# Steps of the second and third token block put in another order (chunked attention followed by an ELU feed-forward, one core)

## The chip, the cores and the metric

The kernel runs on one core of a Trainium2 chip. The metric is the device time of one execution in microseconds (us), taken as the median of several runs. One more execution was recorded by the hardware profiler; the views of that profile are what is read below.

## The reference

What has to be computed, cut to its core (float32 throughout; 8 batches, 8 heads, 576 positions of 64 numbers, so 4608 tokens of 512 numbers; `w_in` is 512x2048, `w_out` 2048x512):

```
scores = scale * q_c @ k_c.T            # per head, inside chunks of 64 positions
attn   = exp(scores - max(scores))
attn   = attn / (sum(attn) + 1e-9)
x      = (attn @ v_c)                   # written as [4608 tokens, 512]
h      = x @ w_in
g      = where(h > 0, h, exp(min(h, 0)) - 1)
out    = g @ w_out
```

Every float32 product of the feed-forward is made of three matmuls of rounded parts: a high part and a low part of each operand, without low times low. Where the text says that something is "split", its high part is a copy on ScalarE and its low part a subtraction on VectorE or GpSimd.

## The kernel before, in words

**Blocks.** The 4608 tokens are nine blocks of 512 (`TB`). The first three are done plainly: `hidden(f)` computes 128 of the 2048 hidden numbers for all 512 tokens with 12 matmuls of 128x512 into a PSUM tile `h` (two buffers); `elu` turns `h` into `ghi` and `glo`; `second_products()` multiplies those with `w_out` in 12 more matmuls into four PSUM tiles `o`, one step later than `hidden` (the queue behind `second`). `f` runs from 0 to 15 in each block. The other six blocks are done as three pairs with seven products for eight (a Strassen scheme: `Pair`, `PAIR`, `KEPT`). They need sums and differences of token blocks, made by `prepare`: B11, B21, B22 are split parts of x, and T1 to T4 are split differences of x of block three and block four. t1, t2, t3, t4 are the bare differences, T1 to T4 their splits. The ending `a` or `b` on such a name means the first columns up to `T2`, or the rest; a token tile is 128 columns, so `T2 = 256` is two tiles of block four and `T2 = 384` three.

**Attention in between.** While block b is in the feed-forward, the attention of later tokens is worked in tiles of 128 (class `Later`): `turn(0)` and `turn(1)` transpose q and k on VectorE (`qT`, `k_turned`), `score` is 32 small matmuls into the PSUM tile `ps_a`, `less_max` two VectorE steps, `exp` one ScalarE step, `sums` three VectorE steps, `turn_a` two VectorE steps, a ScalarE copy (`unturned`) and four DMAs on SyncE's queue, `times_v` 32 small matmuls into `ps_a`, `keep` a ScalarE copy into `xf`.

**What sets the order.** Each engine runs its instructions in the order in which the code issues them; nothing is moved by a scheduler. That order stands in strings, one letter per step, which the loops read from left to right:

- In blocks one and two: `H` is `hidden(f)`, each `e` one of the four parts of `elu` (1: relu and exp on ScalarE; 2: the combining step on VectorE, line 442; 3: `ghi` on ScalarE; 4: `glo`), `P` the 12 products into `o`, `a` the next step of the tile begun earlier, `n` the next step of the following tile, `S` the storing of the finished block, `X` the splitting of x for the next block into `xhi` and `xlo`.
- In block three (`EVEN`, `ODD`, `THIRD_BLOCK`): `q`, `k` are `turn(0)` and `turn(1)`, `s` score, `m` or `M` less_max, `E` or `F` exp, `z` sums, `h` turn_a, `v` times_v, `x` keep, `l` and `V` the loads of a following tile, `A1` to `A7` loads of weight sums, and `xB11`, `xt1a`, `xT1a` and so on a `prepare`.

A letter that is already done for its tile is skipped. An instruction waits for what it reads and for the space that it writes, and all that stands behind it on its engine waits with it. In block three `glo` runs on GpSimd from f = 2 on. `combine()` is a side job that writes sums of weights to memory, one step at the end of each f.

The lines that the text speaks of: 422 the matmuls, 249 `score`, 257 `times_v`, 439 and 440 relu and exp of `elu`, 442 its combining step, 447 `ghi`, 450 `glo`, 455 and 456 the copy and the DMA of an output, 348 the transpositions of q and k, 358 and 359 `less_max`, 364 `exp`, 369 to 371 `sums`, 377 to 387 `turn_a`, 408 `keep`, 508 and 509 the split inside `combine`, 574 and 575 the split and 580 the difference in `prepare`, 847 and 848 the split of x (`split_next`), 636 and 640 the first steps on a product of a pair.

Of the kernel before, what the change touches and what calls it, by code (L numbers as in the profile page):

```python
# [20 lines left out]
def kernel(  # L21
# [19 lines left out]
    nc = tc.nc  # L41

    B, H, S, D = q.shape
# [4 lines left out]
    P = 128  # L48
    C = 64
    TB = 512  # L50
    NB = NT // TB
    NTT = TB // P
    NK = DM // P
    NF = DFF // P
    SCALE = 1.0 / float(D) ** 0.5
    Q = 32
# [1 line left out]
    NS = (NB - PLAIN) // 2  # L58
    NG = NF // 2
    LAG = 1  # L60
    T2 = TB // 2

    REBIAS = 2.0 ** -112
    LARGEST = float(np.uint32(0x0FEFFFFF).view(np.float32))
# [363 lines left out]
    def hidden(f: int):  # L428
        hi, lo = w_in_slices(f)
        h = ps_h.tile([P, TB], F32, name="h")  # L430
        for kt in range(NK):
            three(h, hi[:, kt, :], lo[:, kt, :], xhi[:, kt, :], xlo[:, kt, :],
                  kt == 0, kt == NK - 1)
        return h

    def elu(h, engine=nc.vector):

        e = gp.tile([P, TB], F32, name="e")
        nc.scalar.activation(out=e, in_=h, func=AF.Relu, scale=-1.0)  # L439
        nc.scalar.activation(out=e, in_=e, func=AF.Exp, scale=-1.0)  # L440
        yield
        nc.vector.scalar_tensor_tensor(  # L442
            out=e, in0=e, scalar=-1.0, in1=h, op0=ALU.add, op1=ALU.max
        )
        yield
        ghi = gp.tile([P, TB], F32R, name="ghi")
        nc.scalar.copy(out=ghi, in_=e)  # L447
        yield
        glo = gp.tile([P, TB], F32R, name="glo")
        engine.tensor_tensor(out=glo, in0=e, in1=ghi.bitcast(F32), op=ALU.subtract)  # L450
        yield ghi, glo

    def copy_out(o, n0: int, src, on_vector: bool):

        (nc.vector.tensor_copy if on_vector else nc.scalar.copy)(out=o, in_=src)  # L455
        nc.sync.dma_start(out=out[n0:n0 + P, :], in_=o)

    def store(blk: int, o_ps):
        for tt in range(NTT):
            o = io.tile([P, DM], F32, name="q_sb" if tt % 2 else "k_sb")  # L460
            copy_out(o, blk * TB + tt * P, o_ps[tt], tt % 2 and blk)

# [8 lines left out]
    PRODUCTS = {1: ("A11", "B11"), 2: ("A12", "B21"), 3: ("S4", "B22"), 4: ("A22", "T4"),  # L471
                5: ("S1", "T1"), 6: ("S2", "T2"), 7: ("S3", "T3")}
    a_dram = dram.tile([NG, P, 2, NA, 2 * P], F32, name="a_dram")
# [86 lines left out]
    def b_operand(name: str):  # L560
        place, i = {"B11": (0, 0), "B21": (0, 1), "T1": (1, 0), "T2": (1, 1), "T4": (2, 0),
                    "B22": (3, 0), "T3": (4, 0)}[name]
# [4 lines left out]
    def prepare(name: str, cols=slice(TB), engine=nc.vector):  # L567


        b11, b21, b12, b22 = [xf[:, t, 2 * k:2 * k + 2, cols] for t in range(2) for k in range(2)]  # L570
        sources = {"B11": b11, "B21": b21, "B22": b22, "T1": b11, "T2": b11, "T3": b12, "T4": b21}
        if name in sources:
# [98 lines left out]
    def o_tiles():  # L671
        return [ps_o.tile([P, DM], F32, name=f"o{tt}") for tt in range(NTT)]
# [46 lines left out]
    def warm(n: int):  # L719
# [19 lines left out]
    )  # L739
    SECOND_BLOCK = (  # L740
# [4 lines left out]
    )  # L745
# [1 line left out]
        "H e e e e P",  # L747
        "H e e e e P",
        "n n H e e e e P",
        "n a a n H n X P e e e e",  # L750
    )

    EVEN, ODD = "l H q k e e e e P", "H s v e x V m E e e z h e P"
    THIRD_BLOCK = {
# [9 lines left out]
    }  # L766
    FIRST_PAIR = (
# [40 lines left out]
    with (  # L808
# [5 lines left out]
        for item in LOADS.split():  # L814
            kind, n = item[0], int(item[1:])
# [26 lines left out]
    ps_early = early.enter_context(  # L842
        tc.tile_pool(name="ps_early", bufs=1, space=bass.MemoryType.PSUM))

    def split_next():
        for kt in range(NK):
            nc.scalar.copy(out=xhi[:, kt], in_=xf[:, 0, kt])
            nc.vector.tensor_tensor(  # L848
                out=xlo[:, kt], in0=xf[:, 0, kt], in1=xhi[:, kt].bitcast(F32), op=ALU.subtract)
# [19 lines left out]
    combining = combine()  # L869
# [3 lines left out]
    for blk in range(PLAIN - 1):  # L873
        if blk == 1:
            early.close()
            ps_a = ctx.enter_context(
                tc.tile_pool(name="ps_a", bufs=1, space=bass.MemoryType.PSUM))
        run = blk * TB, o_tiles(), None
        for f in range(NF):
            tt, st = divmod(f, 4)  # L880
            n = (blk + 1) * NTT + tt + 1
            if st == 0:
                if (blk, tt) == (1, 0):
                    following = later[2 * NTT].steps()
                tile_now, following, begun = following, iter(()), 0
                if blk:
                    next(tile_now, None)
                    next(tile_now, None)
                    if tt == 0:
                        later[n] = Later(n)  # L890
                        later[n].load_qk()
                    later[n].load_v()
                    following = later[n].steps()
            lines = FIRST_BLOCK if blk == 0 else SECOND_BLOCK if (blk, tt) == (1, 0) else LATER
            for item in lines[st].split():
                if item == "H":
                    if blk == 0:
                        split_upto(f)
                        if f == NF - 1:
                            kept_st += [stp.tile([P, STAGE], F32, name="kept", tag="st")  # L900
                                        for _ in range(3)][::-1]
                            later[2 * NTT] = Later(2 * NTT)
                            later[2 * NTT].load_qk()
                            later[2 * NTT].load_v()
                    act, acted = elu(hidden(f)), 0
                elif item == "e":
                    g, acted = next(act), acted + 1
                    if acted == 4:
                        second(f, *g)
                elif item == "a":  # L910
                    next(tile_now, None)
                    begun += 1
                    if begun == 2 and n < 2 * NTT:
                        following = early_tile(n)
                elif item == "n":
                    next(following, None)
                elif item == "d":
                    next(splitting, None)
                elif item == "r":
                    next(preparation, None)  # L920
                elif item == "X":
                    if f == NF - 1:
                        split_next()
                elif item == "P":
                    if blk or f:
                        second_products()
                elif item == "S":
                    store(*unstored.pop())
            if (blk or f > 1) and (not blk or f < 2):
                write_lo((f - 2) % NF)  # L930
            if blk:
                next(combining, None)
                if st == 2:
                    later[n + 1] = Later(n + 1)
                    later[n + 1].load_qk()

    n = PLAIN * NTT
    attention = Tokens(later[n], later[n + 1])
    attention.done |= {(n, item) for item in "qksmEV"}

    def do(item: str):
        if item == "Q":
            second_next()
        elif item == "P":
            second_products()
        elif item == "S":
            store(*unstored.pop())
        elif item[0] == "x" and len(item) > 1:
            if preparing:
                name, cols = item[1:3], slice(TB)  # L950
                if item[1] == "B":
                    name = item[1:4]
                elif item[3:4] in ("a", "b"):
                    cols = slice(T2) if item[3] == "a" else slice(T2, TB)
                prepare(name, cols)
        elif item[0] == "A":
            load_a(0, int(item[1]))
        else:
            attention.step(item)
# [3 lines left out]
    for f in range(NF):  # L963
        for item in THIRD_BLOCK.get(f, ODD if f % 2 else EVEN).split():
            if item == "H":
                act, acted = elu(hidden(f), nc.gpsimd if f > 1 else nc.vector), 0
            elif item == "e":
                g, acted = next(act), acted + 1
                if acted == 4:
                    second(f, *g)  # L970
            else:
                do(item)
        next(combining, None)

    plain.close()
    late = ctx.enter_context(tc.tile_pool(name="late", bufs=1, reuse_waits="tile"))
# [65 lines left out]
```

## Time and profile before

| | us |
|---|---|
| median of 3 runs | 852.32 |
| the runs | 850.17, 852.32, 852.5 |
| the profiled execution | 851.5 |
| its span, first to last instruction | 849.7 |

TensorE (PE) is busy 98% of the span, its weight loads (PEld) 80%, VectorE (DVE) 59%, ScalarE (ACT) 57%, GpSimd (POOL) 21%. Block two runs from about 132.5 to 227.4 us of the span, block three from 227.4 to 327.2 us, then the pairs follow. TensorE's granted clock is 0.996 of full speed on average, and 1.00 from 141 to 460 us.

In the views a row of the timeline begins with the start and the duration in us, then engine, line, operation and tiles; a bracket at its end tells for how long the engine was idle just before and what ended that. A 128x512 matmul is listed with 0.39 us, but they overlap: what counts is the distance from one start to the next.

### The profile page before, as it was taken

How to read it: one execution, taken by the hardware profiler on the slowest of the kernel's cores; microseconds unless marked ns; L12 is line 12 of the kernel's file. 1: busy time of each engine (PE TensorE's matmuls, PEld its weight loads, DVE VectorE, ACT ScalarE, POOL GpSimd, SP SyncE). 2: the span in 40 equal slices, each digit the busy share in tenths (PEclk: the TensorE clock that was granted, in tenths of full speed). 3: DMA queues.
4: the chain of work that ended last, by engine and by line, in shares of the span. 5: the costliest groups of instructions: out<-in, count | busy, mean ns of one | idle time of the engine just before them, and what ended most of it. 6: DMA issues, size and time to landing. Idle time of an engine off the chain costs nothing.

```text
span 849.7 us, 15732 instructions
## 1 busy us (share of the span) xinstructions
PE 829.9 (98%) x5959; PEld 677.4 (80%) x5959; DVE 501.4 (59%) x718; ACT 482.0 (57%) x853; POOL 177.3 (21%) x149
## 2 busy tenths in 40 slices
PE   7799999999989999999999999999999999999998
PEld 6688787888768878888888888888887888888786
DVE  5798896666766578666565755666645333233411
ACT  6799985444454446756666436666664355555521
POOL 0000005255302111211112531111125211111120
PEclk9899999999999999999999999999999999999999
DMA  9877672766776785688888666798844365545231
GB/s 240 258 228 227 224 203 79 227 208 224 248 214 177 201 237 165 195 239 248 235 253 260 167 168 198 196 248 252 236 145 147 104 196 158 168 143 161 91 108 49
DMA packets 178794, 164.09 MB, mean 193 GB/s; under 512 B 65568, under 2 KB 161312, under 8 KB 178720
## 3 DMA queue, kind: packets, MB, share of 16 engines
q1 hardware_dynamic: 178720, 163.10, 65.6%
q8 instruction: 47, 0.77, 0.4%
q14 instruction: 27, 0.22, 0.1%
HBM read 131.07 MB, written 28.31 MB: 188 GB/s over the span
## 4 chain that ended last, share of the span: by engine, by line
PE 78%; issue 8%; DVE 5%; ACT 3%; DMA 2%; POOL 2%; SPq 1%; POOLq 0%; ACTq 0%; DVEq 0%
PE o L422 38%; PE h L422 35%; PE ps_a L249 2%; POOL glo L450 2%; PE ps_a L257 1%; PE ps_a L316 1%; DMA kept<-in_q_dram 1%; DVE e L442 1%; DVE kept L509 1%; ACT e L440 1%; DMA k_sb<-in_k_dram 0%; ACT e L439 0%; DMA a_dram<-kept 0%; DVE g_kept L590 0%; PE ps_a L271 0%
## 5 line engine op out<-in xcount | busy, mean ns | idle before, releaser
L422 PE MATMUL o<-wo_hi,ghi 128*128 128x512 f32 x416 | 165.4, 397 | 0.5 <-ACT k_sb L455 0.3
L422 PE MATMUL o<-wo_hi,glo 128*128 128x512 f32 x416 | 163.0, 392 | 1.1 <-DVE glo L450 0.5
L422 PE MATMUL o<-wo_lo,ghi 128*128 128x512 f32 x416 | 162.4, 390 | 0.0
L597 POOL TENSOR_TENSOR glo<-e,ghi 128x512 fp32r<-128x512 f32 x46 | 59.6, 1296 | 310.5 <-ACT ghi L595 310.5
L422 PE MATMUL h<-xhi,wi_hi 128*128 128x512 f32 x336 | 112.1, 392 | 0.6 <-DVE xlo L414 0.6
L422 PE MATMUL h<-xlo,wi_hi 128*128 128x512 f32 x336 | 111.4, 390 | 0.7 <-DVE xlo L848 0.7
L422 PE MATMUL o<-wo_hi,wo_lo 128*128 128x512 f32 x320 | 99.9, 390 | 1.1 <-DVE kept L455 1.1
L422 PEld LDWEIGHTS o<-wo_hi,glo 128*128 128x128 f32 x416 | 78.3, 188 | 19.8 <-DVE glo L450 2.0
L422 PEld LDWEIGHTS o<-wo_hi,ghi 128*128 128x128 f32 x416 | 78.3, 188 | 18.3 <-ACT ghi L447 0.9
L422 PEld LDWEIGHTS o<-wo_lo,ghi 128*128 128x128 f32 x416 | 78.4, 188 | 15.6
L636 ACT COPY kept<-h 128x512 f32<-128x512 f32 x72 | 42.2, 586 | 61.2 <-PE h L422 61.1
L422 PE MATMUL h<-wi_lo,wi_hi 128*128 128x512 f32 x288 | 75.1, 396 | 0.0
L422 PE MATMUL h<-xhi,wi_lo 128*128 128x512 f32 x192 | 74.8, 389 | 0.0
L422 PEld LDWEIGHTS h<-xhi,wi_hi 128*128 128x128 f32 x336 | 63.1, 188 | 14.1 <-PE ps_a L724 0.8
L422 PEld LDWEIGHTS h<-xlo,wi_hi 128*128 128x128 f32 x336 | 63.1, 188 | 14.0 <-DVE xlo L848 1.1
L422 PE MATMUL h<-wo_lo,wi_hi 128*128 128x512 f32 x288 | 73.0, 389 | 0.0
L422 PEld LDWEIGHTS o<-wo_hi,wo_lo 128*128 128x128 f32 x320 | 60.1, 188 | 14.5 <-DVE kept L455 1.9
L590 DVE SCALAR_TENSOR_TENSOR g_kept<-e,g_kept 128x512 f32<-128x512 f32 x48 | 35.5, 739 | 57.5 <-ACT e L587 57.5
L640 DVE TENSOR_TENSOR g_kept<-h,kept 128x512 f32<-128x512 f32 x48 | 33.0, 687 | 51.7 <-ACT kept L636 27.2
L422 PEld LDWEIGHTS h<-wo_lo,wi_hi 128*128 128x128 f32 x288 | 54.0, 188 | 11.3
L587 ACT ACTIVATE e<-e 128x512 f32<-128x512 f32 x96 | 60.7, 633 | 3.1
L422 PE MATMUL o<-wo_lo 128*128 128x512 f32 x160 | 62.3, 389 | 0.0
(108 smaller groups left out, 1319.8 us busy)
## 6 DMA issues: line engine op xcount, KB each, us to landing
wi_hi<-a_dram SPq DMA_DIRECT2D x168, 256.0 KB, 3.7
wo_lo<-lo_dram SPq DMA_DIRECT2D x52, 512.0 KB, 4.9
kept<-in_q_dram SPq DMA_DIRECT2D x100, 128.0 KB, 3.6
kept<-in_k_dram SPq DMA_DIRECT2D x100, 128.0 KB, 4.0
st<-in_moe_w_in_dram SPq DMA_DIRECT2D x16, 512.0 KB, 4.7
v_sb<-in_v_dram SPq DMA_DIRECT2D x32, 256.0 KB, 5.9
st<-in_moe_w_out_dram SPq DMA_DIRECT2D x16, 512.0 KB, 5.2
a_dram<-kept SPq DMA_DIRECT2D x16, 512.0 KB, 3.8
```

The costliest lines, as they stand in the source:

```text
L249: nc.tensor.matmul(scores[halves[c], j, hp, :], lhsT=qT[halves[j], hp, halves[c]], rhs=kT[halves[j], hp, halves[c]], start=True, stop=True,)
L257: nc.tensor.matmul(x_ps[halves[j], c, hp, :], lhsT=v_sb[halves[c], 2 * hp + j, :], rhs=aT[halves[c], :, j * NK + hp], start=True, stop=True,)
L316: nc.tensor.matmul(turned_ps[half, h, :], lhsT=a[half, h, :], rhs=ident[half, half], start=True, stop=True,)
L422: nc.tensor.matmul(ps, lhsT=a, rhs=b, start=start, stop=stop, skip_group_check=onto)
L440: nc.scalar.activation(out=e, in_=e, func=AF.Exp, scale=-1.0)
L442: nc.vector.scalar_tensor_tensor(out=e, in0=e, scalar=-1.0, in1=h, op0=ALU.add, op1=ALU.max)
L450: engine.tensor_tensor(out=glo, in0=e, in1=ghi.bitcast(F32), op=ALU.subtract)
L587: nc.scalar.activation(out=e, in_=e, func=AF.Exp, scale=-1.0)
L590: nc.vector.scalar_tensor_tensor(out=to, in0=e, scalar=-1.0, in1=c, op0=ALU.add, op1=ALU.max)
L597: engine.tensor_tensor(out=lo, in0=e, in1=hi.bitcast(F32), op=ALU.subtract)
L636: nc.scalar.copy(out=c21 if i == 4 else self.kept[i - 1], in_=x_ps)
L640: nc.vector.tensor_tensor(out=to, in0=y_ps, in1=self.kept[kept], op=ALU.add)
```

## The change

Five things, all in the order of issue or in sizes:

1. Block two, tile 0, f = 1: the `turn_a` step of that tile (`a`) moves from ahead of `hidden(1)` to between the second and the third part of `elu`.
2. Block two, f = 15 (`LAST`): the split of x for block three is issued in two pieces, its first quarter before relu and the other three after part 2 of `elu`; the attention's exp comes after them, and `sums` of that tile, which stood in block three, is done here.
3. Block three, f = 0 and 1: `turn_a` first, then `hidden`; the four output tiles are copied by ScalarE (before: two by ScalarE, two by VectorE), and all parts of `elu` come before `times_v`. The step of `combine` moves from the end of every f to the letter `C` in the even ones, so that its last two steps (with lines 508 and 509 in the first of them) come at f = 2 and f = 4.
4. Block three, even f: part 2 of `elu` stands between the two transpositions.
5. The preparations: B11 and B21 at the end of f = 8 and 10 (before: of 9 and 11); the `a` parts cover three tiles (384 columns) and stand at f = 13 and 14 (before: 256 columns, at f = 12 and 14), the `b` parts cover 128 columns. `glo` of f = 15 is VectorE's (before: GpSimd's).

```
-    T2 = TB // 2
+    T2 = TB - P
...
-            copy_out(o, blk * TB + tt * P, o_ps[tt], tt % 2 and blk)
+            copy_out(o, blk * TB + tt * P, o_ps[tt], False)
...
     SECOND_BLOCK = (
         "H e e e e P a a S",
-        "a a a H e e e e P",
+        "a a H e e a e e P",
...
-        "n a a n H n X P e e e e",
+        "n a a n H n P e e e e",
     )
+    LAST = "n a a n H X0 e e X1 X2 X3 P n e n e"
...
-    EVEN, ODD = "l H q k e e e e P", "H s v e x V m E e e z h e P"
+    EVEN, ODD = "l H e q e k e C e P", "H s v e x V m E e e z h e P"
     THIRD_BLOCK = {
-        0: "l V z H h q k e e e e P S",
-        1: "H s e M F P v x V e e z h e",
-        8: "A1 A2 l H q k e e e e P",
-        9: "A3 A4 H s v e x V m E e e z h e xB11 P",
-        10: "A5 A6 l H q k e e e e P",
-        11: "A7 H s v e x V m E e e z h e xB21 P",
-        12: "l H q k e xt1a e e xT1a xt3a e P",
-        14: "l H q k e xt2a e e xT2a xt4a e P",
+        0: "h H e e P l V e S q k e",
+        1: "H s e M P e F e e v x V z h",
+        8: "A1 A2 l H e q e k e e xB11 P",
+        9: "A3 A4 H s v e x V m E e e z h e P",
+        10: "A5 A6 l H e q e k e e xB21 P",
+        11: "A7 H s v e x V m E e e z h e P",
+        12: "l H e q e k e e P",
+        13: "H s v e x V m E e e z h e xt1a P",
+        14: "l H e q e xT1a k e e xt3a xt2a xT2a xt4a P",
         15: "H s v e x V e xt1b xt3b xT1b e xt2b xT2b e xt4b",
     }
...
-    attention.done |= {(n, item) for item in "qksmEV"}
+    attention.done |= {(n, item) for item in "qksmEVz"}
...
-                act, acted = elu(hidden(f), nc.gpsimd if f > 1 else nc.vector), 0
+                act, acted = elu(hidden(f), nc.gpsimd if 1 < f < NF - 1 else nc.vector), 0
...
-        next(combining, None)
```

TensorE's own instructions are the same and in the same order; what moves is on the engines that feed it. (In the lines of the new kernel the split of x is 849 and 850.)

Place one, ScalarE at f = 1 of block two, from the attention's exp on. Before:

```order
L364 ACTIVATE ps_a<-ps_a 128x2x256
L383 COPY unturned<-turned 128x512
L439 ACTIVATE e<-h 128x512
L440 ACTIVATE e<-e 128x512
L447 CAST ghi<-e 128x512
```

and now:

```order
L364 ACTIVATE ps_a<-ps_a 128x2x256
L439 ACTIVATE e<-h 128x512
L440 ACTIVATE e<-e 128x512
L383 COPY unturned<-turned 128x512
L447 CAST ghi<-e 128x512
```

The copy `unturned`, which waits for VectorE's `turn_a`, has gone behind relu and exp of `elu`.

Place two, VectorE from f = 0 of block three to the second half of f = 1. Before, from the transpositions of f = 0 on (the second `L442` is that of f = 1, the `L450` behind `L380` its `glo`):

```order
L348 STREAM_TRANSPOSE k_turned<-kept 128x4x4x32
L442 SCALAR_TENSOR_TENSOR e<-e,h 128x512
L450 TENSOR_TENSOR glo<-e,ghi 128x512
L455 COPY q_sb<-o_1590 128x512
L455 COPY q_sb<-o_1592 128x512
L509 TENSOR_TENSOR kept<-kept 128x1024
L358 TENSOR_REDUCE mx<-ps_a 128x8
L359 TENSOR_TENSOR ps_a<-ps_a,mx 128x2x256
L442 SCALAR_TENSOR_TENSOR e<-e,h 128x512
```

and now, from `turn_a` on, which stands ahead of them:

```order
L380 STREAM_TRANSPOSE turned<-ps_a 128x8x2x32
L442 SCALAR_TENSOR_TENSOR e<-e,h 128x512
L348 STREAM_TRANSPOSE qT<-kept 128x4x4x32
L348 STREAM_TRANSPOSE k_turned<-kept 128x4x4x32
L450 TENSOR_TENSOR glo<-e,ghi 128x512
L358 TENSOR_REDUCE mx<-ps_a 128x8
L359 TENSOR_TENSOR ps_a<-ps_a,mx 128x2x256
L442 SCALAR_TENSOR_TENSOR e<-e,h 128x512
L450 TENSOR_TENSOR glo<-e,ghi 128x512
```

The two copies and the step of `combine` no longer stand ahead of `mx`; the combining step of f = 0 has moved ahead of both transpositions, and `glo` of f = 1 ahead of the next `sums`.

Place three, VectorE from f = 14 of block three to the first step on a pair. Before (the last `L442` is that of f = 15):

```order
L348 STREAM_TRANSPOSE k_turned<-kept 128x4x4x32
L580 TENSOR_TENSOR xf<-xf 128x2x256
L442 SCALAR_TENSOR_TENSOR e<-e,h 128x512
L575 TENSOR_TENSOR wo_lo<-xf,wo_lo 128x2x256
L580 TENSOR_TENSOR xf<-xf 128x2x256
L442 SCALAR_TENSOR_TENSOR e<-e,h 128x512
L580 TENSOR_TENSOR xf<-xf 128x2x256 x2
```

and now:

```order
L442 SCALAR_TENSOR_TENSOR e<-e,h 128x512
L575 TENSOR_TENSOR wo_lo<-xf,wo_lo 128x2x384
L348 STREAM_TRANSPOSE k_turned<-kept 128x4x4x32
L580 TENSOR_TENSOR xf<-xf 128x2x384 x2
L575 TENSOR_TENSOR wo_lo<-xf,wo_lo 128x2x384
L580 TENSOR_TENSOR xf<-xf 128x2x384
L442 SCALAR_TENSOR_TENSOR e<-e,h 128x512
L580 TENSOR_TENSOR xf<-xf 128x2x128 x2
L575 TENSOR_TENSOR wo_lo<-xf,wo_lo 128x2x128
L580 TENSOR_TENSOR xf<-xf 128x2x128
L575 TENSOR_TENSOR wo_lo<-xf,wo_lo 128x2x128
L450 TENSOR_TENSOR glo<-e,ghi 128x512
```

More of the preparation, in longer instructions, stands ahead of the last `L442`, and `glo` of f = 15 has come onto VectorE behind the short ones.

More of the change, by code (lines that the diff above doesn't have):

```diff
@@ L843, with split_next @@
         tc.tile_pool(name="ps_early", bufs=1, space=bass.MemoryType.PSUM))
-    def split_next():
-        for kt in range(NK):
+    def split_next(*kts):
+        for kt in kts or range(NK):
             nc.scalar.copy(out=xhi[:, kt], in_=xf[:, 0, kt])
@@ L894 @@
             lines = FIRST_BLOCK if blk == 0 else SECOND_BLOCK if (blk, tt) == (1, 0) else LATER
-            for item in lines[st].split():
+            for item in (LAST if blk and f == NF - 1 else lines[st]).split():
                 if item == "H":
@@ L920 @@
                     next(preparation, None)
-                elif item == "X":
+                elif item[0] == "X":
                     if f == NF - 1:
-                        split_next()
+                        split_next(*[int(kt) for kt in item[1:]])
                 elif item == "P":
@@ L938 @@
     attention = Tokens(later[n], later[n + 1])
-    attention.done |= {(n, item) for item in "qksmEV"}
+    attention.done |= {(n, item) for item in "qksmEVz"}
     def do(item: str):
-        if item == "Q":
+        if item == "C":
+            next(combining, None)
+        elif item == "Q":
             second_next()
```

## The prediction

> **What bounds the kernel now.** I read the page first, then the chain of waits of TensorE cut to blocks two and three, then TensorE's timeline at each wait, and last the timelines of the engines that it waited for.
>
> ```profile
> span 849.7 us, 15732 instructions
> PE 829.9 (98%) x5959; PEld 677.4 (80%) x5959; DVE 501.4 (59%) x718; ACT 482.0 (57%) x853; POOL 177.3 (21%) x149
> ```
>
> TensorE is the bound: 98% busy. The change leaves its instructions and their order alone, so it can only take waits away or add some. The waits from 141 to 327 us, by who ended them, begin with
>
> ```profile
> PE ps_a L257 <- ACT ps_a L364: 1.5, 1, 1.5
> PE o L422 <- DVE glo L450: 0.5, 1, 0.5
> ```
>
> This list counts idle time only. A late operand also shows as a longer distance between starts, so I measure each place from start to start. Twelve matmuls on an undisturbed stretch take 2.72 us (the row at 155.54 below), 0.227 each.
>
> ```profile
> 147.72 0.39 PE L422 MATMUL h<-xhi,wi_lo 128*128 128x512 f32 x1
> 149.30 0.39 PE L422 MATMUL o<-wo_hi,ghi 128*128 128x512 f32 x1
> ...
> 229.90 0.39 PE L422 MATMUL h<-xhi,wi_lo 128*128 128x512 f32 x1
> 231.29 0.40 PE L422 MATMUL o<-wo_hi,ghi 128*128 128x512 f32 x1
> ...
> 237.17 0.50 PE L422 MATMUL o<-wo_hi,ghi 128*128 128x512 f32 x1 [0.32 <-ACT k_sb L455]
> 241.87 0.79 PE L257 MATMUL ps_a<-turned,v_sb 64*64 64x64 f32 x32 [1.53 <-ACT ps_a L364]
> 245.72 0.39 PE L422 MATMUL o<-wo_lo,ghi 128*128 128x512 f32 x1
> 246.99 0.39 PE L422 MATMUL o<-wo_hi,ghi 128*128 128x512 f32 x1
> ...
> 302.10 0.40 PE L422 MATMUL o<-wo_lo,ghi 128*128 128x512 f32 x1
> 302.54 0.50 PE L422 MATMUL o<-wo_hi,glo 128*128 128x512 f32 x1
> ...
> 314.62 0.40 PE L422 MATMUL o<-wo_lo,ghi 128*128 128x512 f32 x1
> 315.84 0.40 PE L422 MATMUL o<-wo_hi,ghi 128*128 128x512 f32 x1
> ```
>
> The prizes: at 148 us 1.58 - 4 x 0.227 = 0.67; at 230 us 1.39 - 0.91 = 0.48; at 237 us 0.32; at 242 us 1.53; at 246 us 1.27 - 0.45 = 0.82; at 302 us 0.44 - 0.23 = 0.21; at 315 us 1.22 - 0.45 = 0.77. Together 4.80 us: that is all that these edits can win here, whatever they do. Elsewhere the steps are the old ones.
>
> **Part by part. Block two, f = 1 (the wait at 148 us).** The chain that ended last there:
>
> ```profile
> 145.04 0.62 ACT unturned L383
> 145.66 0.51 ACT e L439
> 146.19 0.64 ACT e L440
> 146.85 0.70 DVE e L442
> 147.57 0.63 ACT ghi L447
> ...
> 155.54 2.72 PE o L422 x12
> ```
>
> relu stood behind `unturned`, although `hidden(1)` was through some 24 matmuls before 147.72, at 142.3, plus 0.39 for the last. Now relu and exp go first, from 142.7 to 144.0; VectorE's step of 0.70 to 144.7; then `turn_a`, which takes VectorE some 1.4, to 146.1; `unturned` to 146.7, and `ghi` to 147.3. The products can start at 147.95. Price 0, prize 0.67; the cover is 0.6 us, and a longer `turn_a` would eat it. Moved with it: the four DMAs of `turned`, about 1.0 later, and behind them on SyncE's queue the loads of the next tile, which the next transposition needs only after 169 us.
>
> **Block change and block three, f = 0 and 1.** Rows for the costs (VectorE's and ScalarE's groups from 224 to 260 us, means in ns):
>
> ```profile
> 224.46 0.39 PE L422 MATMUL h<-xhi,wi_lo 128*128 128x512 f32 x1
> 230.81 0.69 DVE L369 TENSOR_REDUCE ps_a<-ps_a 128x8 f32<-128x512 f32 x1
> 232.73 0.72 DVE L380 STREAM_TRANSPOSE turned<-ps_a 128x512 f32<-128x512 f32 x1
> L348 DVE STREAM_TRANSPOSE k_turned<-kept 128x512 f32<-128x512 f32 x3 | 3.2, 1081 | 0.0
> L848 DVE TENSOR_TENSOR xlo<-xf,xhi 128x512 fp32r<-128x512 f32 x4 | 2.5, 688 | 1.2 <-ACT xhi L847 1.2
> L455 ACT COPY k_sb<-o 128x512 f32<-128x512 f32 x2 | 1.1, 584 | 0.0
> ```
>
> `hidden(15)` of block two ends at 224.85. Before, the exp and four casts of x stood ahead of its relu; now one cast, which is done by then. relu 0.6 and exp 0.64 end at 226.1, so `ghi` (after three casts and the attention's exp, 0.6 each at most) is there by 229, ahead of the products at 230.12: the 0.48 goes.
>
> VectorE then: the last `xlo` at 228.7 (three casts of 0.63 after 226.1, and 0.69), `sums` to `turned` 2.64 (230.81 to 233.45), with `glo` of 0.69 between: about 231.9. `unturned` 0.62, relu 0.51, exp 0.66, line 442 0.70: 234.4. Both transpositions are now behind that: 2 x 1.08 less some overlap, 236.1 to 236.5. The score wants `k_turned` after 224.46 + 0.23 + 36 x 0.227 = 232.85 plus one `hidden`, 2.72: 235.6. **Here a new wait appears**, 0.5 to 0.85; I take 0.6. What is late next hangs on the same chain: the products start about 236.9, their banks are free by 236.8 (four copies of 0.58 behind `ghi`), `glo` is there at 236.8, and the attention's exp ends about 239.0, while `times_v` comes at 239.8. So the 0.32 and the 1.53 go, but with only 0.8 of cover. VectorE has lost two copies and `combine`'s step ahead of `mx`, and ScalarE gained two copies, 1.2 us, that are part of this sum. `glo` of f = 1 ends near 240.3 and is wanted at 243.5: the 0.82 goes.
>
> `combine`'s step at f = 2 falls where VectorE waits for the next score; price 0.
>
> **Even f in block three.**
>
> ```profile
> 259.35 1.09 DVE L348 STREAM_TRANSPOSE k_turned<-kept 128x512 f32<-128x512 f32 x1
> 264.07 0.69 PE L249 MATMUL ps_a<-k_turned,qT 64*64 64x64 f32 x32
> 246.70 2.41 SPq L387 DMA_DIRECT2D turned<-unturned  x4
> ```
>
> `k_turned` ended at 260.44, 3.6 us ahead of its score; behind exp and line 442 it ends some 1.6 later. Price 0, cover 2.0. On SyncE the four `turned` DMAs (2.41 to issue) now stand ahead of tile 14's loads at f = 0, which shifts those by about 3 us; they are wanted at f = 2, some 12 us after the issue. `turned` at f = 1 is issued from about 244.4 to 246.8 and wanted at 249.2; its landing is the nearest call on that queue, price 0 to 0.3, taken as 0.
>
> **B parts and T parts, f = 8 to 15.** B11 and B21 now come behind `k_turned` and `glo`, not ahead of the next relu: the waits at 302 and 315 us, both for GpSimd's `glo`, go (0.21 + 0.77). The T parts cost:
>
> ```profile
> 309.20 1.22 DVE L575 TENSOR_TENSOR wi_lo<-xf,wi_lo 128x1024 fp32r<-128x1024 f32 x1 [1.64 <-ACT wi_lo L574]
> 313.70 0.65 PE L257 MATMUL ps_a<-turned,v_sb 64*64 64x64 f32 x32
> 314.17 1.28 POOL L450 TENSOR_TENSOR glo<-e,ghi 128x512 fp32r<-128x512 f32 x1 [7.35 <-ACT ghi L447]
> 314.65 1.35 DVE L575 TENSOR_TENSOR wo_lo<-xf,wo_lo 128x512 fp32r<-128x512 f32 x1 [1.20 <-ACT wo_lo L574]
> 316.52 0.68 DVE L358 TENSOR_REDUCE mx<-ps_a 128x8 f32<-128x512 f32 x1
> 320.56 0.72 DVE L380 STREAM_TRANSPOSE turned<-ps_a 128x512 f32<-128x512 f32 x1
> ...
> 330.78 1.52 PE L422 MATMUL h<-wi_lo,wi_hi 128*128 128x512 f32 x6
> 333.27 0.39 PE L422 MATMUL o<-wo_hi,glo 128*128 128x512 f32 x1
> ```
>
> A two-tile part (512 numbers a partition) takes 0.69 and 1024 numbers 1.22, so three tiles take about 0.95 and one tile 0.4 (estimates between these rows). `times_v` ends at 314.35, `keep` at 315.0, so `mx` starts near 315.1 and not 316.5, and `turned` ends near 319.9. VectorE then: t1a 320.8, `qT` 321.7, line 442 (behind exp) 322.4, T1a (behind its cast) 323.4, `k_turned` 324.4, t3a and t2a 326.2, T2a behind a cast of 0.83 328.0, t4a 328.9, line 442 of f = 15 329.5, six short ones and `glo` 332.7. TensorE, without the 0.77: the second product of the pair needs the space that line 442 frees at 330.78 - 0.77 = 330.0; the first product with `glo` of f = 15 comes at 332.5. So a wait of 0.2 at the least; the row at 314.65 says more: that instruction was under way 1.35 instead of 0.69 while GpSimd's `glo` ran to 315.45, and ended 0.55 after it. GpSimd's `glo` of f = 14 falls from 323.0 on into T1a and t3a, which can shift all by about 0.25. I take 0.45 (0 to 1.0).
>
> The Trainium skill (SBUF — State Buffer, "SBUF: two separate sides") says that VectorE, with two SBUF inputs, and GpSimd hold one port pair by an exclusive lock for a whole instruction, so that the loser is blocked, not slowed. By that rule the wait here is 0.45; without it, it would be 0.2, and the total 0.25 better. The row at 314.65 bears the rule out.
>
> **Sum.** 4.80 - 0.6 - 0.45 = 3.75. The profiled execution took 851.5, 0.8 below the median of the three runs (852.32) and inside them: 851.5 - 3.75 = 847.7 us. Were there no new waits, 846.7; with both at their upper ends, 848.5.
>
> **Rivals.** *The T parts become the bound of the block's end.* Each of the six three-tile instructions at 1.35 instead of 0.95 gives 2.4 us more, and beyond the 0.5 of slack at 330.0 it goes onto TensorE, with `glo` behind: gain 3.75 - 2.2 = 1.5, 850.0. For it: a chain of 13 us on VectorE with casts of ScalarE between; against: only one `glo` of GpSimd falls into it.
>
> *The wait at 242 us comes back.* If score or ScalarE's four copies run 2.0 later than worked out, the 0.8 of cover goes and 1.2 is waited for again, with `k_turned`'s wait above it: gain about 1.9, 849.6. For it: seven steps on two engines in series; against: each has its row.
>
> *Slower:* `k_turned` behind line 442 is late in every even step, seven scores from f = 3 to f = 15. It decides from 2.0 us on; for a loss of 2.6 it would have to add (3.75 + 2.6) / 7 = 0.9 a time, so be 2.9 later than worked out: 854.1. Against it: relu there starts when `unturned` is through, in this trace as in the new order, so nothing moves the exp by that much.
>
> **How the numbers follow.** Forecast 0.70, T parts 0.12, the wait come back 0.10, slower 0.04, something else 0.04. 0.3% is 2.6 us, about what this kernel's runs (850.17 to 852.5) can tell from no change. The forecast's own range is 846.3 to 849.2. The first two rivals lie within 0.3%, so: faster 0.75, same 0.19, slower 0.06. The range goes from 845.8 (no new wait and a run at the low end) to 850.2.
>
> **What would show it.** Right: TensorE's waits between 141 and 327 us no longer name line 364 or GpSimd's `glo`; one names `k_turned` (line 348) at about 235, half a microsecond; one VectorE's `glo` or line 442 right at the start of the pairs. Wrong: a wait for line 364 or 455 at 237 to 242 us, waits at every score, or over 1 us at the first products of the pairs.

## The result and the profile after

| | before | after |
|---|---|---|
| median of 6 runs each, us | 852.41 | 847.75 |
| the runs | 850.17 to 853.35 | 846.65 to 849.45 |
| the profiled execution | 851.5 | 848.72 |
| its span | 849.7 | 846.7 |

The ratio is 0.995, with a 95% interval from 0.9935 to 0.9965: 3.0 to 5.5 us faster. 847.7 was forecast. A second measurement (`e10_after` below) gave 0.9955 (0.9938 to 0.9973).

The page of the kernel after, its span and busy times:

```profile
span 846.7 us, 15737 instructions
PE 829.1 (98%) x5959; PEld 678.1 (80%) x5959; DVE 501.2 (59%) x717; ACT 483.7 (57%) x855; POOL 176.5 (21%) x148
```

TensorE's waits of the kernel after from 141 to 345 us (us in total, times, the longest):

```profile
PE ps_a L249 <- DVE k_turned L348: 0.5, 1, 0.5
PE o L422 <- DMA wi_hi<-a_dram: 0.2, 1, 0.2
```

Lines 364 and 455 and GpSimd's `glo` have left the list. One wait for `k_turned` has come, and one at the start of the pairs, which the view puts down to a DMA; the runs show below that it is VectorE's `glo`.

TensorE's timeline of the kernel after, at four of the places (the start of an undisturbed group of small matmuls comes 0.32 after the matmul ahead of it, and the matmul behind one is followed after 0.34):

```profile
148.82 0.39 PE L422 MATMUL o<-wo_hi,ghi 128*128 128x512 f32 x1
149.05 0.39 PE L422 MATMUL o<-wo_lo,ghi 128*128 128x512 f32 x1
149.27 0.39 PE L422 MATMUL o<-wo_hi,glo 128*128 128x512 f32 x1
...
235.94 0.39 PE L422 MATMUL h<-xhi,wi_lo 128*128 128x512 f32 x1
236.87 0.69 PE L249 MATMUL ps_a<-k_turned,qT 64*64 64x64 f32 x32 [0.54 <-DVE k_turned L348]
...
240.14 0.39 PE L422 MATMUL o<-wo_hi,glo 128*128 128x512 f32 x1
240.46 0.69 PE L257 MATMUL ps_a<-turned,v_sb 64*64 64x64 f32 x32
...
329.57 0.39 PE L422 MATMUL o<-wo_lo,ghi 128*128 128x512 f32 x1
330.13 0.50 PE L422 MATMUL o<-wo_hi,glo 128*128 128x512 f32 x1 [0.18 <-DMA wi_hi<-a_dram]
330.47 0.86 PE L422 MATMUL h<-wo_lo,wi_hi 128*128 128x512 f32 x3
```

At 148 us the steps are 0.23: no wait. The score comes 0.93 after the matmul ahead of it, 0.61 more than undisturbed. `times_v` comes after 0.32. The last of the 12 products at 330 us is 0.56 behind its neighbour and the next matmul 0.34 behind it: (0.56 - 0.23) + (0.34 - 0.23), about 0.45 lost.

Cut at the starts of scores and of `times_v`, which both traces have, the stage reads:

| stretch of before, us | before | after | gained | forecast |
|---|---|---|---|---|
| 139.02 to 151.43 (the wait at 148) | 12.41 | 11.73 | 0.68 | 0.67 |
| 151.43 to 220.73 (rest of block two) | 69.30 | 69.71 | -0.41 | 0 |
| 220.73 to 236.15 (block change, to the score of f = 1) | 15.42 | 15.53 | -0.11 | 0.48 - 0.6 |
| 236.15 to 241.87 (score to `times_v`) | 5.72 | 3.59 | 2.13 | 0.32 + 1.53 |
| 241.87 to 251.87 (with the wait at 246) | 10.00 | 9.01 | 0.99 | 0.82 |
| 251.87 to 300.67 (four more tiles) | 48.80 | 48.80 | 0 | 0 |
| 300.67 to 313.19 (302) | 12.52 | 12.20 | 0.32 | 0.21 |
| 313.19 to 326.15 (315) | 12.96 | 12.20 | 0.76 | 0.77 |
| the start of the pairs | | | -0.45 | -0.45 |

Together 3.91, against 3.75 forecast. The span is shorter by 3.0 only: the score that stands at 139.02 before stands at 139.90 after, 0.88 later, ahead of all that was changed. The granted clock was lower there (from the start: stretch, its length, TensorE's busy time, clock, DMA share, GB/s). Before:

```profile
20.00:40.00 20.00, 14.91 (x205) 0.85 0.92 267
40.00:60.00 20.00, 20.00 (x147) 0.98 0.69 206
```

and after:

```profile
20.00:40.00 20.00, 15.35 (x206) 0.81 0.93 271
40.00:60.00 20.00, 20.00 (x143) 0.93 0.63 194
```

That goes the same way, but it need not be all of it: `e3_parts` below was granted 0.89 and 0.94 in these stretches, as much in sum as before, and reached this score at 139.78.

### The profile page after: what moved, and what is told of

Read it like the earlier page. It is cut to its first block, busy times and chain, and to the rows that moved or that the text cites. A ratio compares the mean times of both kernels' runs of the same rounds, so it can differ in the third digit from the quotient of the medians.

```text
span 846.7 us, 15737 instructions
## 1 busy us (share of the span) xinstructions
PE 829.1 (98%) x5959; PEld 678.1 (80%) x5959; DVE 501.2 (59%) x717; ACT 483.7 (57%) x855; POOL 176.5 (21%) x148
## 4 chain that ended last, share of the span: by engine, by line
PE 90%; ACT 3%; DMA 2%; DVE 2%; SPq 1%; issue 1%; DVEq 0%; ACTq 0%
PE o L422 44%; PE h L422 41%; PE ps_a L249 2%; PE ps_a L257 2%; SPq L213 1%; DMA k_sb<-in_k_dram 1%; PE ps_a L316 1%; DMA v_sb<-in_v_dram 1%; DMA wi_hi<-a_dram 1%; DMA turned<-unturned 0%; DVE g_kept L590 0%; PE ps_a L271 0%; ACT e L440 0%; ACT e L587 0%; DVE xlo L850 0%
```

## Experiments

The theory was the prediction's: each place gains by itself, the two new waits come from `k_turned` behind line 442 and from VectorE's late `glo`. The rivals were that the parts lean on each other, that the new waits come from something else (a DMA, the length of the T parts), and that the covers are thinner or thicker than worked out. Since executions differ by 2 us or more ahead of block two, single runs are judged by the places in their traces, and only the two kernels with five rounds by their times. The runs come from several chips: beside e1, e2, e3 and e6 the kernel before took 851.96 in its one run, beside e4, e5, e7 and e9 it took 849.90.

### One part alone, on the kernel before

`e1_turn_a_later`, part 1 alone:

```
-        "a a a H e e e e P",
+        "a a H e e a e e P",
```

> The kernel before, with the first edit alone (turn_a between the parts of elu at f = 1 of block two). Theory (relu stood behind the copy of turn_a): from the last matmul of the hidden at 147.7 us to the fourth into o takes 0.91 and not 1.58, so 0.67 less; every other wait of the kernel before stays (0.48 at 230, 1.53 at 242, 0.77 at 315 us). Rival (the four DMAs of turned, about 1.0 later, now end last): a new wait of 0.2 to 0.7 at times_v near 152 us, gain under 0.5. The whole time moves by less than this run can tell.

851.44, beside 851.96 for the kernel before on the same chip. TensorE's timeline at the place:

```profile
148.13 0.39 PE L422 MATMUL o<-wo_hi,ghi 128*128 128x512 f32 x1
148.36 0.39 PE L422 MATMUL o<-wo_lo,ghi 128*128 128x512 f32 x1
```

A step of 0.23, and 11.73 us from score to score as in the kernel after: the whole prize of that place. Of the waits that were to stay, the one at 230 us came out smaller: the block change took 15.24 us here, 0.18 less than in the trace of before with the same code. In the list from 141 to 327 us line 364 keeps its 1.5, and two more read:

```profile
PE ps_a L257 <- DMA wi_hi<-a_dram: 0.6, 1, 0.6
PE o L422 <- POOL glo L450: 0.5, 1, 0.5
```

The first is new, a `times_v` at 301.13. It needs `turned`, whose four transfers (KB each, median us from issue to landing; the stretch from 290 to 302 us) took in this run

```profile
turned<-unturned SPq DMA_DIRECT2D x4, 32.0 KB, 5.3
```

and in the trace of before

```profile
turned<-unturned SPq DMA_DIRECT2D x4, 32.0 KB, 3.7
```

They are issued from 295.06 to 297.53 and wanted at 300.4. That ate the 0.67 in this one execution. The code of that stretch is the old one, so I read it as a landing that scatters; `e3_parts` shows it once more, smaller.

`e2_block_change`, parts 2 and 3 alone, with the even steps otherwise in the old order:

```
+    LAST = "n a a n H X0 e e X1 X2 X3 P n e n e"
-    EVEN, ODD = "l H q k e e e e P", ...
+    EVEN, ODD = "l H q k e e e C e P", ...
-        0: "l V z H h q k e e e e P S",
-        1: "H s e M F P v x V e e z h e",
+        0: "h H e e P l V e S q k e",
+        1: "H s e M P e F e e v x V z h",
...  (output copies on ScalarE, split_next in pieces, combine by "C")
```

> The kernel before, with the second and third edit alone (split of x and sums at the end of block two, turn_a first, all four copies on ScalarE, combine's last steps at f = 2 and 4). Theory: the waits at 230, 237, 242 and 246 us go (0.48 + 0.32 + 1.53 + 0.82) and one for k_turned of 0.6 comes; from the first matmul of hidden(0) to that of hidden(2) in block three 13.1 us, as in the changed kernel, and not 15.2. The waits at 148, 302 and 315 us stay. Rival (the new order of the even f carries part of it): more than 13.5 us, with a wait at times_v.

850.88 (before 851.96). TensorE's timeline from the first matmul of `hidden(0)` to that of `hidden(2)`:

```profile
228.66 0.39 PE L422 MATMUL h<-xhi,wi_hi 128*128 128x512 f32 x1
...
237.53 0.69 PE L249 MATMUL ps_a<-k_turned,qT 64*64 64x64 f32 x32 [0.55 <-DVE k_turned L348]
...
241.75 0.50 PE L422 MATMUL h<-xhi,wi_hi 128*128 128x512 f32 x1
```

13.09 us, as after (13.07) and not as before (15.19): the block change gains its part without the others, and brings the wait for `k_turned` with it. The waits at 148, 302 and 315 us stay (0.5 for GpSimd's `glo`). At 213 us this run lost 0.62 that no other shows; its cause stands in the last section.

`e3_parts`, parts 4 and 5 alone:

```
-    T2 = TB // 2
+    T2 = TB - P
-    EVEN, ODD = "l H q k e e e e P", ...
+    EVEN, ODD = "l H e q e k e e P", ...
...  (lines 8 to 14 of THIRD_BLOCK as in the change; glo of f = 15 on VectorE)
```

> The kernel before, with the fourth and fifth edit alone (line 442 between the two transpositions, B parts one step earlier, T parts for three tiles, last glo on VectorE). Theory: the waits for GpSimd's glo at 302 and 315 us (0.21 + 0.77) go, a wait of 0.45 comes at the first product with glo of f = 15; the waits at 148, 230, 237, 242 and 246 us stay. Rival (the wait at the block's end comes from the steps of f = 0 and 1, which shift the loads): no wait at the block's end here.

851.41 (before 851.96). No wait names GpSimd any more, and the products at 302 and 315 us follow undisturbed. The stretch with the place at 302 us took 12.39, though, and not the 12.20 of the kernel after: 0.2 is lost inside `times_v`, whose 32 matmuls took 0.84 and not 0.65.

```profile
301.83 0.84 PE L257 MATMUL ps_a<-turned,v_sb 64*64 64x64 f32 x32
302.61 0.50 PE L422 MATMUL o<-wo_hi,ghi 128*128 128x512 f32 x1
```

It is the same `times_v` that waited in e1, and its four transfers of `turned` took 4.3 us here (median from issue to landing), against 3.7 before, 3.6 after and 5.3 in e1. At the start of the pairs:

```profile
332.81 0.39 PE L422 MATMUL o<-wo_lo,ghi 128*128 128x512 f32 x1
333.36 0.50 PE L422 MATMUL o<-wo_hi,glo 128*128 128x512 f32 x1 [0.17 <-DMA wi_hi<-a_dram]
```

0.55 behind its neighbour, 0.56 in the kernel after, and 0.23 in e2, which has the old preparations: the loss belongs to these two parts.

### The new wait for `k_turned`

`e6_turn_a_behind_exp`, on the kernel after:

```
-        0: "h H e e P l V e S q k e",
+        0: "H e h e P l V e S q k e",
```

> The changed kernel, with turn_a of f = 0 in block three issued behind relu and exp (H e h e instead of h H e e). Theory (the score waits for k_turned since relu stands behind the copy unturned): exp ends some 2 us earlier, k_turned 1.8 earlier, and the distance from the last matmul of hidden(1) to the score goes from 0.93 back to 0.32. Rival (the transpositions wait for the loads of q and k or for VectorE's other work): 0.9 stays. Second rival (turned lands later): a new wait at times_v.

847.32. ScalarE's `unturned`, which waits for VectorE's `turned`, no longer stands ahead of relu and exp. VectorE's and TensorE's timelines:

```profile
232.88 1.07 DVE L348 STREAM_TRANSPOSE k_turned<-kept 128x512 f32<-128x512 f32 x1
```

```profile
235.04 0.39 PE L422 MATMUL h<-xhi,wi_lo 128*128 128x512 f32 x1
235.35 0.69 PE L249 MATMUL ps_a<-k_turned,qT 64*64 64x64 f32 x32
```

`k_turned` ends at 233.95, 1.4 ahead of its score, and the score follows after 0.31. From `times_v` of block two's last tile to this score it is 14.41, against 15.02 after: the full 0.61, and it is not lost again at `times_v`, which follows after 0.32.

`e4_copies_back`, two of the output copies back on VectorE:

```
-            copy_out(o, blk * TB + tt * P, o_ps[tt], False)
+            copy_out(o, blk * TB + tt * P, o_ps[tt], tt % 2 and blk)
```

> The changed kernel, with two of the four output copies of a block back on VectorE. Theory: they stand ahead of the two transpositions of f = 0 and delay them by 1.2, so the distance from the last matmul of hidden(1) to the score grows from 0.93 to about 2.1, and TensorE loses 1.2 us there. Rival (ScalarE's four copies are what delays, since the attention's exp stands behind them): with two of them gone ScalarE is 1.0 earlier and the distance stays at 0.9 or shrinks.

848.54. VectorE and TensorE:

```profile
233.79 1.28 DVE L455 COPY q_sb<-o 128x512 f32<-128x512 f32 x2
```

```profile
237.15 0.69 PE L249 MATMUL ps_a<-k_turned,qT 64*64 64x64 f32 x32 [1.73 <-DVE k_turned L348]
```

`qT`, which would have begun at 233.79, begins behind them at 234.99, and the wait grows from 0.54 to 1.73, by 1.19: nothing is left there that could take up a delay of VectorE.

`e5_combine_early`, the step of `combine` at f = 0 and 1 instead of in the even f:

```
-    EVEN, ODD = "l H e q e k e C e P", ...
+    EVEN, ODD = "l H e q e k e e P", ...
-        0: "h H e e P l V e S q k e",
-        1: "H s e M P e F e e v x V z h",
+        0: "h H e e P l V e S q k e C",
+        1: "H s e M P e F e e v x V z h C",
```

> The changed kernel, with combine's last two steps back at the end of f = 0 and f = 1 of block three. Theory (the wait of 1.53 for the attention's exp came from what stood ahead of mx on VectorE and ahead of relu on ScalarE): the step's 1.06 on ScalarE and 1.23 on VectorE put mx near 239.6 instead of 237.6, exp ends near 241.5, and times_v, wanted at 240.5, waits 1.0 to 1.2. Rival (the 2.7 us of products between score and times_v cover it): no wait at times_v.

848.29. VectorE, and TensorE at `times_v`:

```profile
237.04 1.23 DVE L509 TENSOR_TENSOR kept<-kept 128x1024 fp32r<-128x1024 f32 x1 [1.12 <-ACT kept L508]
238.18 0.68 DVE L358 TENSOR_REDUCE mx<-ps_a 128x8 f32<-128x512 f32 x1
```

```profile
240.33 0.58 PE L257 MATMUL ps_a<-turned,v_sb 64*64 64x64 f32 x19 [1.14 <-ACT ps_a L364]
```

The wait for line 364, the largest of the kernel before, is back: score to `times_v` takes 4.78 instead of 3.59, 1.2 more. So the place of `combine`'s step carries over half of what that stretch won (2.13).

### The new wait at the start of the pairs

`e7_glo_earlier`, the same preparations with the fourth part of `elu`, `glo`, three instructions sooner (and the third, `ghi`, ahead of `t1b`):

```
-        15: "H s v e x V e xt1b xt3b xT1b e xt2b xT2b e xt4b",
+        15: "H s v e x V e e xt1b xt3b e xT1b xt2b xT2b xt4b",
```

> The changed kernel, with ghi and glo of f = 15 ahead of T1b, t2b and T2b. Theory (the matmul at 330.1 us waited for VectorE's glo, behind those): glo ends near 328.3 and the 0.45 there falls to 0.1 or less; T2b and the copy of the first product now end just in time, at 330.0. Rival (it waited for the landing of a weight-sum load, line 540, which the profile names there): the 0.45 stays.

VectorE's `glo` and TensorE's products:

```profile
325.04 0.69 DVE L450 TENSOR_TENSOR glo<-e,ghi 128x512 fp32r<-128x512 f32 x1
```

```profile
327.03 0.39 PE L422 MATMUL o<-wo_lo,ghi 128*128 128x512 f32 x1
327.25 0.39 PE L422 MATMUL o<-wo_hi,glo 128*128 128x512 f32 x1
```

A step of 0.22, and the next matmul begins at 327.50: at this place the 0.45 is gone, with SyncE's loads of `wi_hi` in the same order. The DMA that the view named was not the cause; in the kernel after VectorE's row says it too, 329.39 + 0.68 = 330.07 against a start at 330.13:

```profile
329.39 0.68 DVE L450 TENSOR_TENSOR glo<-e,ghi 128x512 fp32r<-128x512 f32 x1
```

More than half of the prize is lost again within 4 us. The matmuls at 327.84 and 330.71 come 0.34 behind their neighbours, where the kernel after has 0.24 and 0.23, and from `times_v` to the second of these it is 10.06 us, against 10.25 after: 0.19 stays won. Both neighbours, at 327.50 and 330.37, begin 0.05 behind the end of a copy of ScalarE that takes a product of the pair out of PSUM (line 636, ends at 327.45 and 330.32); the expectation had the first of these copies ending just in time. That these copies are the next limit is read from the rows; no run moved them.

The run's 845.61 is not owed to this alone: its xlo wait of block two came 2.7 us sooner than in the kernel after; its granted clock was 1.00 from 20 to 60 us (last section).

`e9_two_tiles`, whether three tiles matter:

```
-    T2 = TB - P
+    T2 = TB // 2
```

> The changed kernel with T2 = 256 again: a parts of two tiles, b parts of two. Theory (VectorE's work adds up along the chain, so the split of it matters little): line 442 of f = 15 ends 1.3 earlier, the b parts take 1.4 more, glo of f = 15 ends within 0.3 of the place it has with three tiles, and the wait at the first product with it is 0.45, between 0.2 and 0.7. Rival (the third tile in the a parts makes VectorE late): the wait is gone. Second rival (three tiles are needed): the wait is over 1.0.

848.36. VectorE's last split before `glo`, and TensorE:

```profile
327.60 0.69 DVE L575 TENSOR_TENSOR wo_lo<-xf,wo_lo 128x512 fp32r<-128x512 f32 x1 [0.69 <-ACT wo_lo L574]
```

```profile
328.95 0.50 PE L422 MATMUL o<-wo_hi,glo 128*128 128x512 f32 x1 [0.35 <-DMA wi_hi<-a_dram]
```

The product comes 0.73 behind its neighbour, 0.17 more than with three tiles: the `b` parts ahead of `glo` take 0.69 instead of 0.43. So the third tile ahead is worth 0.17, and the wait is there either way.

### All together

`e10_after` is the kernel after once more, and `e8_all` the two repairs (e6 and e7) and one more move: in the last f of block one the split of x for block two (`X`) stands ahead of the last two parts of `elu`, and not behind them.

```
+    FIRST_LAST = "r H d a e d d e r a X e d d e d P d"
-        0: "h H e e P l V e S q k e",
+        0: "H e h e P l V e S q k e",
-        15: "H s v e x V e xt1b xt3b xT1b e xt2b xT2b e xt4b",
+        15: "H s v e x V e e xt1b xt3b e xT1b xt2b xT2b xt4b",
-            for item in (LAST if blk and f == NF - 1 else lines[st]).split():
+            for item in ((LAST if blk else FIRST_LAST) if f == NF - 1 else lines[st]).split():
```

> The changed kernel again, beside the next one on the same chip. Expected: 0.995 of the kernel before, between 0.993 and 0.997.

> The changed kernel with three more moves of the same kind: turn_a of f = 0 behind exp, ghi and glo of f = 15 ahead of T1b, and the split of x at the end of block one ahead of ghi and glo there. Theory: the waits of 0.61 for k_turned, 0.45 for glo and 1.0 for the first xlo of block two (0.73 idle and the late start behind it) go, 2.0 us in all, 0.24% of the time: 0.9975 of the changed kernel, about 845.7. Rival (a wait removed there comes back at the next stage, since stores, loads and the pairs keep their own times): under 0.8 us, and new waits in the trace after those places.

| one chip (11, 5 and 6 runs) | median, us | runs | ratio to before (95%) |
|---|---|---|---|
| before | 852.84 | 849.47 to 854.03 | |
| `e10_after` | 847.98 | 847.68 to 850.27 | 0.9955 (0.9938 to 0.9973) |
| `e8_all` | 845.81 | 843.67 to 846.91 | 0.9921 (0.9903 to 0.9939) |

`e8_all` has no wait of TensorE in the list from 110 to 345 us. `e10_after` has three there, the one for `k_turned` and

```profile
PE h L422 <- DVE xlo L850: 0.7, 1, 0.7
...
PE o L422 <- DVE glo L450: 0.2, 1, 0.2
```

TensorE at the start of block two in `e8_all`, a step of 0.23 to the first matmul that needs `xlo`, where `e10_after` has 1.12:

```profile
130.23 0.39 PE L422 MATMUL h<-xhi,wi_hi 128*128 128x512 f32 x1
130.46 0.39 PE L422 MATMUL h<-xlo,wi_hi 128*128 128x512 f32 x1
```

The places are worth 0.86 (10.07 to 9.21 us from `times_v` to score), 0.61 and about 0.2 (the steps of 0.33 behind e7's place are here too, though no wait is listed), together 1.7; the medians differ by 2.17. So the 2.0 that was expected came out with one of its three terms less than half as large, and some 0.5 stands without a place. The intervals of the two ratios just touch, but all six runs of `e8_all` lie below all five of `e10_after`; both are faster than before. `e8_all` has the lowest median of the versions that were run more than once.

## Why the prediction was right

**The prizes.** All seven waits went, and e1, e2 and e3 show that each part takes its own at its places. The size was a little low: 0.67 + 0.48 + 0.32 + 1.53 + 0.82 + 0.21 + 0.77 = 4.80 stood in the sum, and the table gives 0.68 + 0.50 + 2.13 + 0.99 + 0.32 + 0.76 = 5.38 (0.50 is -0.11 with the 0.61 taken out). The step at fault is the one that took single late starts for the whole wait. TensorE's timeline of before, between the score and `times_v`:

```profile
237.74 0.40 PE L422 MATMUL o<-wo_hi,glo 128*128 128x512 f32 x1
238.01 0.50 PE L422 MATMUL o<-wo_hi,ghi 128*128 128x512 f32 x1
238.34 0.39 PE L422 MATMUL o<-wo_lo,ghi 128*128 128x512 f32 x1
```

The product at 238.01, the first into the second `o` tile, was late too, by 0.04 and 0.11 behind it; the products at 237.17 came 1.02 after the score and not 0.63 (0.39, I had 0.32), and `times_v` 1.91 after the product ahead of it and not 0.32 (1.59, I had 1.53). That is 2.13. The 0.50 is less firm: with the same old code the block change took 15.42 in the trace of before, 15.24 in e1 and 15.22 in e3, so the wait at 230 us was worth 0.3 there. At 302 us I left out the matmul behind the wait, which is followed after 0.34 and not 0.23: the 0.11 that were missing.

**The wait for `k_turned`.** 0.6 forecast, 0.61 measured. The chain was right as well: `xlo`, `sums`, `turned`, `unturned`, relu, exp, line 442, two transpositions. e6 shows that the wait hangs on `unturned` ahead of relu, and e4 that any more work of VectorE there adds in full.

**The cover at `times_v`.** 0.8 forecast. In the kernel after ScalarE's exp ends 0.73 ahead of `times_v`:

```profile
239.15 0.58 ACT L364 ACTIVATE ps_a<-ps_a 128x512 f32<-128x512 f32 x1 [0.59 <-DVE ps_a L359]
```

The rival in which this wait comes back asked for 2.0 of delay and gave 1.2 for it. In e5 the exp ended 4.72 after the score began, in the kernel after 2.86: with 1.86 of delay 1.2 came back, so the rival's price was right and only its cause was missing here.

**The even steps.** `k_turned` ends 1.86 to 1.93 ahead of its score at f = 4 to 12, 2.0 was forecast; 1.38 at f = 2 and 0.96 at f = 14, with T1a ahead of it. All those scores follow undisturbed, so the slower rival had no place to begin.

**The T parts.** 0.95 was estimated for three tiles and 0.4 for one; VectorE's rows of the kernel after are

```profile
319.75 0.96 DVE L575 TENSOR_TENSOR wo_lo<-xf,wo_lo 128x768 fp32r<-128x768 f32 x1
...
321.56 1.99 DVE L580 TENSOR_TENSOR xf<-xf 128x768 f32<-128x768 f32 x2
...
327.69 0.43 DVE L575 TENSOR_TENSOR wo_lo<-xf,wo_lo 128x256 fp32r<-128x256 f32 x1
```

GpSimd's `glo` of f = 14 ran from 320.51 for 1.36. T1a and the transposition behind it took their usual time beside it; only the first of the two at 321.56 was held, and took 1.12 instead of 0.95. So GpSimd cost 0.17 where 0.25 was taken; the wait was 0.45 all the same, in part by luck: 0.34 of it is the late start, and the 0.11 behind it stood in no term. That rival, 850.0, needed six long ones.

**What was not foreseen.** The rest of block two lost 0.41 in the profiled execution, nearly all of it (0.38) in the tile with 190 us. "Elsewhere the steps are the old ones" failed there, in this execution: e5, e6 and e9, with the same code in that stretch, took 69.24, as e1 did with the old one. It nearly cancels what the prizes were short of: 3.91 against 3.75.

**What was luck.** The waits were foreseen one by one; that the median came out at 847.75, so close to 847.7, is luck. The sum was taken from one profiled execution, 851.5, and the median of the six runs of before lies 0.9 above that. The medians differ by 4.66, the places of this pair of traces by 3.91, the two profiled executions by 2.8, and no trace shows where the rest of the 4.66 lies.

## What to carry to other kernels

A wait that is read from idle time is short by the steps around it, so measure from one start to the next across the place, in a stretch that both kernels have, and let the stretch end some us behind it: e7's place gained 0.45 and 3 us later 0.19. When part of an engine's work is moved ahead of a wait, ask what the order leaves in front of the steps that TensorE wants next: here one copy that waited for another engine stood ahead of relu, and swapping two letters won 0.61. Where a view names a transfer as the cause of a wait, look at the rows of the operands: one whose last instruction ends just ahead of the late start is the better suspect, and moving that one instruction settles it.

## What the runs showed of the hardware

**A wait that comes and goes.** In block two `glo` of VectorE meets GpSimd's additions of `combine` (line 480), which start when a DMA has landed, so at another time in each execution. Kernel after, VectorE and GpSimd:

```profile
182.42 1.38 DVE L450 TENSOR_TENSOR glo<-e,ghi 128x512 fp32r<-128x512 f32 x1 [0.69 <-ACT ghi L447]
```

```profile
180.71 2.55 POOL L480 TENSOR_TENSOR kept<-wi_hi,wi_lo 128x512 f32<-128x512 f32 x2 [3.96 <-DMA a_dram<-kept]
```

`glo` ended 0.54 after GpSimd's pair of additions, as the row of before at 314.65 did by 0.55. What follows on VectorE is late by as much: `sums`, `turned`, and one step later the `ghi` and `glo` that TensorE wants at 190 us. The same `glo` took 0.87 in the traces of before and of e9, with no wait, 1.42 in e10's, with 0.42 lost, and 1.66 in e7's, with 0.56. In e2 one of the next tile took 1.77, and TensorE lost 0.62:

```profile
205.78 1.77 DVE L450 TENSOR_TENSOR glo<-e,ghi 128x512 fp32r<-128x512 f32 x1 [0.69 <-ACT ghi L447]
```

The Trainium skill (SBUF — State Buffer, "SBUF: two separate sides") has the one that starts first hold the shared pair of ports for its whole instruction; these rows agree, since VectorE's end follows GpSimd's by half a microsecond however early it began. All twelve traces say the same: of VectorE's `glo` from 130 to 222 us, 82 took over 0.70, and each of them ended 0.55 behind the end of one of GpSimd's additions. And the loss goes by the end of `glo`, not by its length. Take the two tiles whose scores stand at 174.51 and 197.59 before, and the time from that score to the end of the `glo` that begins some 7.5 us behind it. Twelve traces give 24 such times: up to 8.46 us TensorE lost 0.01 at most, at 8.66 0.04, at 8.80 0.17, at 9.00 0.38, at 9.19 0.56 and at 9.25 0.62, that is, all that goes beyond about 8.62. That a later landing alone made the difference was not tried.

**The start.** From 20 to 60 us the granted clock differs between executions. e7 and e8 were granted 1.00 throughout and are the earliest at block two, here e7 (its row from 40 to 60 us has 1.00 as well):

```profile
20.00:40.00 20.00, 15.27 (x215) 1.00 0.94 264
```

Block two's first wait came at 131.71 in e7 and at 134.45 in the kernel after, with the same code up to there: 2.7 us, more than half of what the change won. The clock does not order the others: e3, granted 0.89 and 0.94, was only 0.1 us ahead of the kernel after, granted 0.81 and 0.93, at the last `times_v` ahead of block two (129.73 and 129.83). A single run of this kernel can't tell a gain of 1 us; the places in its trace can.
